# A fused retention, gated MLP and convolution-gate kernel: a third buffer for one tile, other places for weight decoding, and finer first splits

## The chip, the cores and the metric

The kernel runs on one core of one Trainium2 chip. The metric is the device time of one execution in microseconds, as the median of several runs; the profile is one further execution with the hardware profiler. TensorE is called PE here, VectorE DVE, ScalarE ACT, GpSimd POOL and SyncE SP.

## The reference, cut to what matters

Inputs are float32 `q`, `k`, `v` of 8 batches, 8 heads, 576 positions and 64 head dimensions. Weights are handed to the kernel as pairs of 32-bit words of a double. Three layers follow one another (512 model dimensions, feed-forward width 1024):

```
ret = (scale * q @ k.T) * Dmat            # Dmat: gamma[h] ** (i - j) for i >= j, else 0
x   = heads_to_model(ret @ v)             # 8 x 576 x 512

h   = gelu_tanh(x @ w_in);  u, v = halves(h)
v_n = (v - mean) / sqrt(var + 1e-6) * g_ln
v_s = w_sg @ v_n + b_sg                   # mixes the 576 positions of a batch
x   = x + (u * v_s) @ w_out

gate = sigmoid(causal_conv5(x, conv_w));  val = x @ w_val
out  = (gate * val) @ w_out2
```

## The kernel before, in words

**Products.** Every large product is made of three float32r products of a high and a low part (high by high, high by low, low by high), so each operand is "split": ACT copies it into a float32r tile (`hi`, L71), DVE subtracts that from the original (`lo`, L74). A product over 512 model dimensions is 12 matmuls (`product`, L85 to L91).

**First phase, an order written out by a planner.** Up to L901 the program order is the order on every engine (`manual_schedule`, L97). Retention is computed in groups of 192 positions, three to a batch, 24 in all: a burst "o" (`outputs`) and a burst "s" (`scores`, which also calls `adds`). For each batch b there are slow tiles on PE: 4 or 5 tiles "v" (`v_tile`, L435; 12 matmuls of 512 columns; the fifth, s = 4, only in odd batches, carries the last 64 positions of two batches), 8 tiles "u" (`u_tile`, L490; 12 matmuls of 288 columns) and 8 tiles "m" (`mix` and `mix_rest`, L504 to L527; 14 matmuls of 288 columns). The list `slow` (L842 to L854) begins with the v tiles of batches 0 and 1 (nine in a row), and then goes, for b = 0 to 5, through m of batch b, v of batch b + 2, u of batch b + 2. `PLACES` (L33) says ahead of which of these tiles a burst is put. v, u and m tiles share two PSUM buffers (`ps_g`, L110), so PE can begin a tile only when the tile two before it has been read out.

What follows a v tile is a chain over four engines: `v_gelu` (ACT, L446, into a tile `vt`), `v_stat` (DVE L454, L455, then three small POOL instructions L456 to L458 that make `rs`), `v_norm` (ACT L463, in place on `vt`, needs `rs`), `v_high` (ACT L71, into `vh`, or for s = 4 two casts into `vr`) and `v_low` (DVE L74). The pool `two` (L100) gives `vt` two buffers, so the gelu of v tile s + 2 needs `v_low` of tile s done. A u tile is read out by `u_gelu` (ACT L502), an m tile by `gate` (DVE L534, L538).

`plan` (L762) keeps a virtual time `now`: a v tile adds 2.79, a u tile 1.6, an m tile 1.87, and each following step is an event at `now` plus a constant; `work` (L835) sorts the events by time and emits them in that order. `KEYS` (L39) holds the constants; entries 9 to 11 are the offsets of `v_norm`, `v_high` and `v_low` behind the end of their v tile:

```
at(now + 0.1, v_gelu, *args)
at(now + 0.8, v_stat, *args)
for x, f in enumerate((v_norm, v_high, v_low)):
    at(now + KEYS[9 + x], f, *args)
```

**Decoding of the later weights.** Twelve blocks of 128 x 512 doubles (`w_out`, `w_val`, `w_out2`, four each) are decoded two per batch, for batches 2 to 7. `fetch_second` (SP, called at m tile 4 of the batch two before) loads a block into a ring of two `raw` buffers. `decode_at` (L822) is called behind the first u tile: `begin` does the ACT step L128, then there are 4 + 2 + 2 DVE steps (L130 to L143), and a last step, one ACT copy (L146) and SP's write of the decoded block into the DRAM tile `w2d` (L200). The DVE temporaries come from `small_tmp` (L172), where "a" has two buffers and "s" and "t" have one. `KEYS[4]` to `KEYS[8]` set the offsets: both `begin`s at -6 and -5 (in the v tiles), the DVE steps of both blocks from 1.0 on at every 1.5, the last steps at 8 and 12.5. In the same way `split_w_sg` (L865 to L868) splits the five blocks of `w_sg` among the first nine v tiles; `wr`, the fifth, is read by `mix_rest`.

**Second phase, ordered by a scheduler.** From L904 on a list scheduler orders each engine's instructions by its own model. The 4608 positions are cut into nine blocks of 512. `fetch` loads a block of the gated activations (`graw`) and of x (`xraw`), 1 MB each; `split_g` splits the first; `back` is the product with `w_out` and adds x (L939); `split_x` splits the sum; `conv` is the five-tap convolution and the sigmoid (L956 to L961, 16 DVE steps L958 per block); `value` the product with `w_val` (L969), `final` that with `w_out2` (L980). Blocks 0 and 1 are fetched during the last m tiles (batches 6 and 7, L892 to L901), where the piecewise `split_g(0, i)` stands between `mix_rest` and `gate`. `w_out` (`wo`) and then `w_val` and `w_out2` (the halves of `wv`, 2 MB each) are loaded from `w2d` by POOL's queue (L911 to L915). `final` of the last block copies the two halves of a column by ACT and DVE into one tile `o`, each half with a DMA of its own (L986 to L989).

Of the kernel before, what the change touches and what calls it, by code (L numbers as in the profile page):

```python
# [37 lines left out]

KEYS = (13.0, 2.5, 8.0, 2.0, -6.0, 1.0, 1.5, 8, 4.5, 3.9, 4.7, 5.5)  # L39

# [6 lines left out]
def fused_kernel(  # L47
# [48 lines left out]
    with ExitStack() as p1:  # L96
# [75 lines left out]
        def small_tmp(n):  # L172
            return [dec.tile([128, FH], U32, tag=f"d{x}", name=f"d{x}", bufs=2 if x == "a" else 1)[:, :n] for x in "ast"]

# [269 lines left out]
        def v_gelu(b, s):  # L444
            vt = two.tile([128, FH], F32, tag="vt", name="vt")
            act.activation(vt, vs[b, s][0], AF.Gelu_apprx_tanh)  # L446
            vs[b, s] = [vt]
# [314 lines left out]
        def plan(kind, *args):  # L762
# [29 lines left out]
            elif kind == "v":  # L792
                now += 2.79
                at(start, v_tile, *args)
                at(now + 0.1, v_gelu, *args)
                at(now + 0.8, v_stat, *args)
                for x, f in enumerate((v_norm, v_high, v_low)):
                    at(now + KEYS[9 + x], f, *args)
            elif kind == "u":
# [22 lines left out]
        def decode_at(b, place):  # L822
            d = {}

            def begin(j):
                d[j] = decode_second(j)
                run(d[j], 1)

            for n, j in enumerate(jobs(b)):
                at(place + KEYS[4] + n, begin, j)  # L830
                for x in range(3):
                    at(place + KEYS[5] + KEYS[6] * (3 * n + x), lambda j=j, x=x: run(d[j], (4, 2, 2)[x]))
                at(place + KEYS[7] + KEYS[8] * n, lambda j=j: run(d[j]))

# [42 lines left out]
        def fetch(i):  # L877
            g = q_g.tile([128, KT, BLK], F32, tag="graw", name="graw")
            x = q_r.tile([128, KT, BLK], F32, tag="xraw", name="xraw")
            sync.dma_start(out=g, in_=g1d[:, :, i * BLK : (i + 1) * BLK])  # L880
            sync.dma_start(out=x, in_=x1d[:, :, i * BLK : (i + 1) * BLK])
            blk[i] = dict(g=g, x=x)

# [9 lines left out]
        for b in (B - 2, B - 1):  # L893
            for i in range(2 * KT):
                mix(b, i)
                mix_rest(b, i)
                if b == B - 1 and i < KT:
                    split_g(0, i)
                gate(b, i)
                if (b, i) == (B - 1, KT):  # L900
                    fetch(1)  # L901
# [11 lines left out]
    with tc.issue_after(first.ins):  # L913
        for i in range(2):
            pool.dma_start(out=wv[:, i], in_=w2d[:, i + 1])  # L915
    split_g(1)

# [23 lines left out]
    def split_x(i):  # L941
        t = blk[i]
        t["xs"] = q_s.tile([128, 2, KT, BLK], F32R, tag="xs", name="xs")
        for a, z, o in parts(i):
            src = t["x2"][:, :, a + o : z + o]
            hi(act, t["xs"][:, 0, :, a:z], src)
            lo(t["xs"][:, 1, :, a:z], src, t["xs"][:, 0, :, a:z])

# [28 lines left out]
    def final(i, m):  # L977
        t = blk[i]
        ps = ps_2.tile([128, 512], F32, tag="p2", name="ps_out")
        product(ps, BLK, wv[:, 1], slice(m * 128, m * 128 + 128), t["gv"][:, 0], t["gv"][:, 1], slice(0, BLK))  # L980
        o = q_2.tile([128, BLK], F32, tag="o", name="o")
        if i < NBLK - 1:
            act.copy(o, ps[:, :BLK])
            act.dma_start(out=out[:, m, i * BLK : (i + 1) * BLK], in_=o)
            return
        for h, copy, eng in ((0, act.copy, act), (1, dve.tensor_copy, sync)):  # L986
            part = slice(h * BLK // 2, (h + 1) * BLK // 2)
            copy(o[:, part], ps[:, part])
            eng.dma_start(out=out[:, m, i * BLK + part.start : i * BLK + part.stop], in_=o[:, part])  # L989

# [118 lines left out]
```

## Time and profile before

| what | value |
|---|---|
| median of 3 runs | 746.45 us (745.9 to 747.17) |
| the profiled execution's own time | 748.05 us |
| its span in the trace | 746.3 us |
| PE matmul busy | 712.9 us (96%), 7842 matmuls |
| DVE busy | 517.0 us (69%) |
| ACT busy | 331.0 us (44%) |
| POOL busy | 56.4 us (8%) |
| mean granted clock of PE | 0.991 of full speed |
| DMA | 120.93 MB, mean 162 GB/s |

The span is what lies between the first and the last instruction in the trace; the execution's own time has 1.75 us around it. Busy time of PE is modelled: each matmul's bar overlaps the next one's, so a share of 96% says that PE rarely ran dry, not that it worked at its peak. The chain of waits, followed back from the last instruction, runs over PE for 80% of the span, over DVE for 6% and over ACT for 5%.

### The profile page before, as it was taken

How to read it: one execution, taken by the hardware profiler on the slowest of the kernel's cores; microseconds unless marked ns; L12 is line 12 of the kernel's file. 1: busy time of each engine (PE TensorE's matmuls, PEld its weight loads, DVE VectorE, ACT ScalarE, POOL GpSimd, SP SyncE). 2: the span in 40 equal slices, each digit the busy share in tenths (PEclk: the TensorE clock that was granted, in tenths of full speed). 3: DMA queues.
4: the chain of work that ended last, by engine and by line, in shares of the span. 5: the costliest groups of instructions: out<-in, count | busy, mean ns of one | idle time of the engine just before them, and what ended most of it. 6: DMA issues, size and time to landing. Idle time of an engine off the chain costs nothing.

```text
span 746.3 us, 18098 instructions
## 1 busy us (share of the span) xinstructions
PE 712.9 (96%) x7842; PEld 622.4 (83%) x7842; DVE 517.0 (69%) x903; ACT 331.0 (44%) x635; POOL 56.4 (8%) x123
## 2 busy tenths in 40 slices
PE   3799989999999999999999998999999999999997
PEld 3789779898898998998989986888888888888886
DVE  5777678775766765857846569998685958667422
ACT  5666464552643635427345125464352535243221
POOL 0000340300301103001022000000000000000000
PEclk9699999999999999999999999999999999999999
DMA  8969339487079573383531984440422403010111
GB/s 332 354 235 310 125 102 309 177 270 255 6 227 330 171 257 133 139 291 132 163 112 53 399 296 137 146 169 6 164 67 103 141 29 113 1 56 1 56 57 57
DMA packets 54719, 120.93 MB, mean 162 GB/s; under 512 B 3952, under 2 KB 25584, under 8 KB 53872
## 3 DMA queue, kind: packets, MB, share of 16 engines
q1 hardware_dynamic: 36352, 95.13, 37.2%
q10 hardware_dynamic: 17856, 18.35, 6.9%
q0 software_dynamic: 432, 6.29, 2.2%
q8 instruction: 61, 1.00, 0.5%
q14 instruction: 18, 0.15, 0.1%
HBM read 85.16 MB, written 34.60 MB: 160 GB/s over the span
## 4 chain that ended last, share of the span: by engine, by line
PE 80%; DVE 6%; ACT 5%; issue 3%; DMA 2%; POOL 2%; SPq 1%; DVEq 0%; POOLq 0%; ACTq 0%
PE ps_m L516 14%; PE ps_out L91 13%; PE ps_val L91 13%; PE ps_back L91 12%; PE ps_u L91 10%; PE ps_v L429 6%; PE xo L363 2%; DMA qk_sb<-in_qk 2%; PE sc L285 2%; PE xo L355 2%; PE ps_m L524 2%; PE st L301 2%; ACT vt L463 2%; ACT vt L446 1%; DVE stat L454 1%
## 5 line engine op out<-in xcount | busy, mean ns | idle before, releaser
L516 PE MATMUL ps_m<-ws,vh 128*128 128x288 f32 x768 | 113.9, 297 | 0.6 <-DVE gt L534 0.6
L958 DVE SCALAR_TENSOR_TENSOR gate<-x,cw_sb,gate 128x516 f32<-128x516 f32 (+1 forms) x144 | 103.8, 750 | 6.6 <-ACT gate L956 5.3
L516 PEld LDWEIGHTS ps_m<-ws,vh 128*128 128x128 f32 x768 | 105.0, 188 | 1.9 <-DVE gt L534 0.8
L91 PE MATMUL ps_back<-gs,wo 128*128 128x512 f32 x432 | 102.6, 395 | 1.0 <-ACT gs L71 0.6
L91 PE MATMUL ps_val<-xs,wv 128*128 128x512 f32 x432 | 102.5, 395 | 0.9 <-ACT xs L71 0.9
L91 PE MATMUL ps_out<-gv,wv 128*128 128x512 f32 x432 | 102.3, 395 | 0.0
L91 PEld LDWEIGHTS ps_back<-gs,wo 128*128 128x128 f32 x432 | 80.9, 188 | 21.2 <-ACT gs L71 1.1
L91 PEld LDWEIGHTS ps_val<-xs,wv 128*128 128x128 f32 x432 | 81.2, 188 | 20.5 <-ACT xs L71 1.3
L91 PEld LDWEIGHTS ps_out<-gv,wv 128*128 128x128 f32 x432 | 81.3, 188 | 19.2
L91 PE MATMUL ps_u<-xh,wi 128*128 128x288 f32 x448 | 92.9, 297 | 4.0 <-ACT u L502 3.1
L91 PEld LDWEIGHTS ps_u<-xh,wi 128*128 128x128 f32 x448 | 72.6, 188 | 5.9 <-ACT u L502 3.8
L429 PE MATMUL ps_v<-wi,xh 128*128 128x512 f32 x224 | 70.7, 396 | 1.4 <-ACT vt L446 1.4
L91 PE MATMUL ps_u<-xl,wi 128*128 128x288 f32 x224 | 65.9, 294 | 0.0
L973 DVE TENSOR_TENSOR gvf<-ps_val,gate 128x512 f32<-128x512 f32 (+7 forms) x64 | 26.6, 453 | 47.6 <-PE ps_val L91 47.5
L534 DVE SCALAR_TENSOR_TENSOR gt<-ps_m,g_sb,b_sb 128x288 f32<-128x288 f32 x64 | 33.0, 516 | 32.5 <-PE ps_m L524 32.5
L375 ACT COPY xg<-xo 128x768 f32<-128x768 f32 x24 | 19.1, 798 | 77.7 <-PE xo L363 61.4
L71 ACT CAST gv<-gvf 128x512 fp32r<-128x512 f32 x36 | 22.3, 620 | 65.1 <-DVE gvf L973 64.6
L429 PEld LDWEIGHTS ps_v<-wi,xh 128*128 128x128 f32 x224 | 41.5, 188 | 11.2 <-ACT vt L446 1.8
L446 ACT ACTIVATE vt<-ps_v 128x512 f32<-128x512 f32 x36 | 21.5, 598 | 62.1 <-PE ps_v L429 49.4
L956 ACT ACTIVATE gate<-x,cw_sb 128x516 f32<-128x516 f32 (+1 forms) x36 | 25.8, 724 | 47.7 <-DVE x L939 47.6
L265 ACT ACTIVATE kk_sb<-kk_sb,kf_sb 128x64 f32<-128x64 f32 x184 | 46.7, 336 | 0.4 <-DMA kk_sb<-in_kk 0.4
L454 DVE BATCH_NORM_STATS2 stat<-vt 128x6 f32<-128x512 f32 x36 | 25.0, 693 | 31.6 <-ACT vt L446 31.5
(98 smaller groups left out, 1078.9 us busy)
## 6 DMA issues: line engine op xcount, KB each, us to landing
qk_sb<-in_qk SPq DMA_DIRECT2D x24, 960.0 KB, 7.8
vv_sb<-in_vv SPq DMA_DIRECT2D x24, 576.0 KB, 4.6
kk_sb<-in_kk SPq DMA_DIRECT2D x24, 384.0 KB, 5.2
x1d<-xg ACTq DMA_DIRECT2D x24, 384.0 KB, 6.7
g1d<-u SPq DMA_DIRECT2D x16, 576.0 KB, 6.9
graw<-g1d SPq DMA_DIRECT2D x9, 1024.0 KB, 5.9
xraw<-x1d SPq DMA_DIRECT2D x9, 1024.0 KB, 5.3
out<-o ACTq DMA_DIRECT2D x32, 256.0 KB, 2.0
```

The source lines that it names most:

```text
L71: return act.copy(dst, src) if engine is act else engine.tensor_copy(dst, src)
L91: pe.matmul(ps[:, :n], lhs, rhs[:, k, x_cols], start=i == 0, stop=i == last)
L265: act.mul(k[:, j, n], k[:, j, n], kf_sb[:, j, n : n + 1])
L375: act.copy(t["xc"].rearrange("p (o c) n -> p c o n", o=2), t["xo"][:, :, : 2 * GT].rearrange("p c (o n) -> p c o n", o=2),)
L429: pe.matmul(ps, lhs, rhs, start=i == 0, stop=i == KT * 3 - 1)
L446: act.activation(vt, vs[b, s][0], AF.Gelu_apprx_tanh)
L454: dve.bn_stats(stat, vt)
L516: pe.matmul(ps[:, :n], lhs, rhs, start=first, stop=False)
L534: dve.scalar_tensor_tensor(gt, mx.pop((b, i))[:, :n], g_sb[:, m : m + 1], b_sb[:, t0 : t0 + n], op0=ALU.mult, op1=ALU.add)
L956: act.mul(gt, x2[:, m, a:z], cw_sb[:, m, 0:1])
L958: last = dve.scalar_tensor_tensor(gt, x2[:, m, a + j : z + j], cw_sb[:, m, j : j + 1], gt, op0=ALU.mult, op1=ALU.add)
L973: dve.tensor_tensor(gv[:, a:z], ps[:, a:z], t["gate"][:, m, a + o : z + o], op=ALU.mult)
```

## The change

- `vt` gets three buffers for two (2 KB per partition), and the temporary "a" of `small_tmp` one for two (2 KB less).
- The offsets of `v_norm`, `v_high` and `v_low` become 4.1, 4.9 and 5.7; for a batch's last v tile, from batch 2 on, 5.1, 6.0 and 7.0 (`LAST`).
- The two decodings of a batch no longer overlap: block n of a pair has `begin` at 0.5, its DVE steps at 2.0, 3.5 and 5.0 and its last step at 7.5, all plus 8.1 n, counted from the end of the first u tile.
- In the last m tiles `gate` stands ahead of the piecewise `split_g(0, i)`.
- The load of `w_out2` stands in an `issue_after` block on SP's last fetch of block 1; it no longer stands in the one on the load of `w_out`.
- `split_g(1)` and `split_x(0)` work in four pieces of 512 columns each.
- In the last block, the second half of a column goes through a tile of its own (tag "gvf").

```diff
@@ -36,7 +36,8 @@
     ((1, 7, 10), (1, 7, 12)), ((0, 4, 7), (0, 4, 7)),
 ]
 
-KEYS = (13.0, 2.5, 8.0, 2.0, -6.0, 1.0, 1.5, 8, 4.5, 3.9, 4.7, 5.5)
+LAST = (5.1, 6.0, 7.0)
+KEYS = (13.0, 2.5, 8.0, 2.0, 0.5, 2.0, 1.5, 7.5, 8.1, 4.1, 4.9, 5.7)
 
 
 def _as_f32(bits):
@@ -170,7 +171,7 @@
             )
 
         def small_tmp(n):
-            return [dec.tile([128, FH], U32, tag=f"d{x}", name=f"d{x}", bufs=2 if x == "a" else 1)[:, :n] for x in "ast"]
+            return [dec.tile([128, FH], U32, tag=f"d{x}", name=f"d{x}", bufs=1)[:, :n] for x in "ast"]
 
         raws, mx = {}, {}
 
@@ -442,7 +443,7 @@
             vs[b, s] = [ps]
 
         def v_gelu(b, s):
-            vt = two.tile([128, FH], F32, tag="vt", name="vt")
+            vt = two.tile([128, FH], F32, tag="vt", name="vt", bufs=3)
             act.activation(vt, vs[b, s][0], AF.Gelu_apprx_tanh)
             vs[b, s] = [vt]
 
@@ -794,8 +795,9 @@
                 at(start, v_tile, *args)
                 at(now + 0.1, v_gelu, *args)
                 at(now + 0.8, v_stat, *args)
+                last = args[1] == 3 + args[0] % 2 and args[0] > 1
                 for x, f in enumerate((v_norm, v_high, v_low)):
-                    at(now + KEYS[9 + x], f, *args)
+                    at(now + (LAST if last else KEYS[9:])[x], f, *args)
             elif kind == "u":
                 now += 1.6
                 at(start, u_tile, *args)
@@ -827,10 +829,11 @@
                 run(d[j], 1)
 
             for n, j in enumerate(jobs(b)):
-                at(place + KEYS[4] + n, begin, j)
+                p = place + KEYS[8] * n
+                at(p + KEYS[4], begin, j)
                 for x in range(3):
-                    at(place + KEYS[5] + KEYS[6] * (3 * n + x), lambda j=j, x=x: run(d[j], (4, 2, 2)[x]))
-                at(place + KEYS[7] + KEYS[8] * n, lambda j=j: run(d[j]))
+                    at(p + KEYS[5] + KEYS[6] * x, lambda j=j, x=x: run(d[j], (4, 2, 2)[x]))
+                at(p + KEYS[7], lambda j=j: run(d[j]))
 
         def work(lists):
             for kind, *args in lists:
@@ -878,8 +881,8 @@
             g = q_g.tile([128, KT, BLK], F32, tag="graw", name="graw")
             x = q_r.tile([128, KT, BLK], F32, tag="xraw", name="xraw")
             sync.dma_start(out=g, in_=g1d[:, :, i * BLK : (i + 1) * BLK])
-            sync.dma_start(out=x, in_=x1d[:, :, i * BLK : (i + 1) * BLK])
-            blk[i] = dict(g=g, x=x)
+            last = sync.dma_start(out=x, in_=x1d[:, :, i * BLK : (i + 1) * BLK])
+            blk[i] = dict(g=g, x=x, fetched=last.ins)
 
         def split_g(i, k=None):
             t = blk[i]
@@ -894,9 +897,9 @@
             for i in range(2 * KT):
                 mix(b, i)
                 mix_rest(b, i)
+                gate(b, i)
                 if b == B - 1 and i < KT:
                     split_g(0, i)
-                gate(b, i)
                 if (b, i) == (B - 1, KT):
                     fetch(1)
 
@@ -911,9 +914,11 @@
     first = pool.dma_start(out=wo, in_=w2d[:, 0])
     wv = wbig.tile([128, 2, 2, KT, DM], F32R, tag="wbig", name="wv")
     with tc.issue_after(first.ins):
-        for i in range(2):
-            pool.dma_start(out=wv[:, i], in_=w2d[:, i + 1])
-    split_g(1)
+        pool.dma_start(out=wv[:, 0], in_=w2d[:, 1])
+    with tc.issue_after(blk[1]["fetched"]):
+        pool.dma_start(out=wv[:, 1], in_=w2d[:, 2])
+    for k in range(KT):
+        split_g(1, k)
 
     def parts(i):
 
@@ -941,10 +946,11 @@
     def split_x(i):
         t = blk[i]
         t["xs"] = q_s.tile([128, 2, KT, BLK], F32R, tag="xs", name="xs")
-        for a, z, o in parts(i):
-            src = t["x2"][:, :, a + o : z + o]
-            hi(act, t["xs"][:, 0, :, a:z], src)
-            lo(t["xs"][:, 1, :, a:z], src, t["xs"][:, 0, :, a:z])
+        for m in range(KT) if i == 0 else (slice(None),):
+            for a, z, o in parts(i):
+                src = t["x2"][:, m, a + o : z + o]
+                hi(act, t["xs"][:, 0, m, a:z], src)
+                lo(t["xs"][:, 1, m, a:z], src, t["xs"][:, 0, m, a:z])
 
     def conv(i):
         t = blk[i]
@@ -978,15 +984,16 @@
         t = blk[i]
         ps = ps_2.tile([128, 512], F32, tag="p2", name="ps_out")
         product(ps, BLK, wv[:, 1], slice(m * 128, m * 128 + 128), t["gv"][:, 0], t["gv"][:, 1], slice(0, BLK))
-        o = q_2.tile([128, BLK], F32, tag="o", name="o")
         if i < NBLK - 1:
+            o = q_2.tile([128, BLK], F32, tag="o", name="o")
             act.copy(o, ps[:, :BLK])
             act.dma_start(out=out[:, m, i * BLK : (i + 1) * BLK], in_=o)
             return
-        for h, copy, eng in ((0, act.copy, act), (1, dve.tensor_copy, sync)):
+        for h, copy, eng, tag in ((0, act.copy, act, "o"), (1, dve.tensor_copy, sync, "gvf")):
+            o = q_2.tile([128, BLK], F32, tag=tag, name="o")[:, : BLK // 2]
             part = slice(h * BLK // 2, (h + 1) * BLK // 2)
-            copy(o[:, part], ps[:, part])
-            eng.dma_start(out=out[:, m, i * BLK + part.start : i * BLK + part.stop], in_=o[:, part])
+            copy(o, ps[:, part])
+            eng.dma_start(out=out[:, m, i * BLK + part.start : i * BLK + part.stop], in_=o)
 
     for i in range(NBLK + 2):
         if i < NBLK:
```

## Rows read from the trace of the kernel before

**Rows 1.** PE by stage: stretch, its length, PE busy (matmuls), granted clock, DMA share, GB/s.
```profile
76.00:437.50 361.50, 352.93 (x5071) 1.00 0.57 197
437.50:454.00 16.50, 14.57 (x61) 1.00 0.57 203
454.00:742.20 288.20, 288.20 (x1239) 1.00 0.23 79
742.20:746.30 4.10, 0.00 (x1) 1.00 0.38 130
```
**Rows 2.** The same columns of PE, around its interruptions behind 76 us.
```profile
95.00:100.00 5.00, 3.65 (x17) 1.00 0.23 60
105.00:108.00 3.00, 2.01 (x13) 1.00 0.63 197
141.00:143.00 2.00, 1.72 (x13) 1.00 0.00 0
194.00:202.00 8.00, 6.85 (x49) 1.00 0.01 2
243.00:246.00 3.00, 2.47 (x19) 1.00 0.00 0
398.00:401.00 3.00, 1.99 (x15) 1.00 0.00 0
424.00:428.00 4.00, 3.40 (x26) 1.00 1.07 416
447.00:454.00 7.00, 5.07 (x20) 1.00 0.38 130
```
**Rows 3.** Timeline of PE: start us, us, instructions, [idle before <- releaser].
```profile
98.10 0.39 PE L429 MATMUL ps_v<-wi,xl 128*128 128x512 f32 x1
99.84 0.73 PE L429 MATMUL ps_v<-wi,xh 128*128 128x512 f32 x2 [1.35 <-ACT vt L446]
```
**Rows 4.** Waits of ACT, 76 to 440 us: us in total, times, longest.
```profile
ACT vt L446 <- DVE vh L74: 11.8, 16, 2.0
...
ACT vt L463 <- POOL rs L458: 11.3, 13, 1.4
```
**Rows 5.** Timeline of ACT behind the last v tile of batch 7.
```profile
397.95 0.82 ACT L463 ACTIVATE vt<-vt,rs 128x512 f32<-128x512 f32 x1 [1.14 <-POOL rs L458]
398.80 1.26 ACT L71 CAST vr<-vt 64x512 fp32r<-64x512 f32 x2
```
**Rows 6.** POOL's instruction L457 over the whole span: ns min/median/max.
```profile
L457 POOL TENSOR_TENSOR rs<-rs,nh_sb x36: 569/571/1137, 80.9 to 395.9; 128x1 f32<-128x1 f32 x36
```
**Rows 7.** DVE busy in the second decoding of batch 7, and in the second phase's start.
```profile
402.50:406.60 4.10, 3.41 (x7) 1.00 0.34 128
444.00:506.00 62.00, 60.97 (x90) 1.00 0.41 137
```
**Rows 8.** Waits of PE and POOL over the whole span; issues of the block writes, us to landing.
```profile
PE sc L285 <- DMA qk_sb<-in_qk: 9.0, 2, 8.5
...
POOL wv L915 <- DMA w2d<-raw: 13.5, 1, 13.5
...
w2d<-raw SPq DMA_DIRECT2D x12, 512.0 KB, 4.0
```
**Rows 9.** Timeline of ACT in the last m tiles.
```profile
424.54 1.66 ACT L71 CAST gs<-graw 128x512 fp32r<-128x512 f32 x3 [16.42 <-DMA graw<-g1d]
```
**Rows 10.** Tile graw, 400 to 470 us: ns min/median/max of the splits, both shapes.
```profile
L71 ACT CAST gs<-graw x7: 613/622/1909, 424.5 to 468.9; 128x512 fp32r<-128x512 f32 x4, 128x2048 fp32r<-128x2048 f32 x3
L74 DVE TENSOR_TENSOR gs<-graw,gs x6: 684/690/2293, 425.2 to 460.9; 128x512 fp32r<-128x512 f32 x4, 128x2048 fp32r<-128x2048 f32 x2
```
**Rows 11.** Timelines of ACT and of DVE, the split of block 1.
```profile
447.64 1.89 ACT L71 CAST gs<-graw 128x2048 fp32r<-128x2048 f32 x1
...
450.93 2.29 DVE L74 TENSOR_TENSOR gs<-graw,gs 128x2048 fp32r<-128x2048 f32 x1
```
**Rows 12.** Timeline of DVE at the end.
```profile
742.64 0.42 DVE L988 COPY o<-ps_out 128x256 f32<-128x256 f32 x1 [0.81 <-ACT o L988]
```

## The prediction, written before the changed kernel was run

> **What bounds the kernel now.** I read the windows by stage first, then PE's interruptions, then the waits that cause them. PE is the bound: from 454 to 742.2 us it has no gap, 1239 matmuls in 288.2 us, 0.2326 us each, and from 76 to 437.5 us it is idle 361.50 - 352.93 = 8.57 us; the clock is 1.00, the upper level (2.4 GHz), in all of these [rows 1]. The change removes no matmul. It can win only what PE loses in gaps, and the start before 76 us is not touched, since its order is written out and stays.
>
> The gaps are few [rows 2]: 1.35 us near 99, 0.99 near 106, 0.28 near 142, 1.15 between 194 and 202, 0.53 near 244, 1.01 near 399 (one like it lies near 300), 0.60 near 426, and 1.93 between 447 and 454. A gap costs more than its idle time, because bars overlap: at 98.10 the next matmul begins 1.74 later where 0.233 is the pace, so 1.51 is lost for 1.35 idle, and the pair behind it runs 0.73 - 0.39 = 0.34 apart, another 0.11 [rows 3]. I price each interruption at its idle time plus 0.27.
>
> **Third vt buffer, and later offsets.** In the v tiles ACT's gelu waited 16 times for DVE's low part of the tile two before, 11.8 us [rows 4]; when two PSUM tiles are unread, PE stops. That is the gap at 99, and by the timeline also those at 142 and 244, where the first u tiles wait for the last v gelu. With three buffers that gelu waits for the tile three before, 2.8 us more slack than a wait of 2.0 at most. So the wait goes. Next late is the norm, which waited 13 times, 11.3 us, for POOL's `rs` [rows 4], but with another 2.8 us of cover.
>
> The gap at 106 is `wr`, split late on DVE. By the planner's numbers split k stands at 13.9 + 2.79 k = 2.79 (k + 3) + 5.53: behind the low part of tile k + 2 at offset 5.5, ahead of it at 5.7. The last split so no longer sits behind that wait, and I count the gap as gone: 1.35 + 0.99 idle.
>
> The gaps at 202, 300 and 399 are one pattern: behind a batch's last v tile ACT waits 1.14 for `rs`, then runs two casts of 1.26 together, and the u gelus queued behind them free no PSUM [rows 5]. `LAST` puts the norm behind the third u gelu (5.1 against 4.9), about 1.2 us later, by which time `rs` is there, and casts and norm (0.82 + 1.26 = 2.1 us) end about when the fourth u gelu is wanted. Behind the waiting norm stand that gelu and, with it, the sixth u tile; a remnant of 0.1 to 0.3 us each is possible.
>
> Sum here: idle 1.35 + 0.99 + 0.28 + 1.15 + 0.53 + 2 x 1.01 = 6.32, nine interruptions x 0.27 = 2.43, together 8.75. I keep 0.8 back for remnants: **7.95**. Bounds: 8.75, and half of it if another engine inherits the wait. The remaining 8.57 - 6.32 - 0.60 = 1.65 us of gaps I leave as they are.
>
> **Decodings one by one.** Nothing is added; two ACT steps leave the v tiles, and the second block's eight DVE steps (3.4 us [rows 7]) move to 10.1, 11.6 and 13.1 behind the first u tile. The u tiles end at 7 x 1.6 = 11.2, the first m tile at 13.1; its gate stands behind the last two steps, so ends near 13.1 + 1.1 + 0.5 = 14.7, and the third m tile wants its PSUM at 14.9. DVE has nothing else there and will start the steps as soon as the ACT step is done, so I cost it at nothing; without that cover at most about 1 us a batch, six times. On SP the last block write moves from 12.5 to 15.6. It lands 4.0 us after issue [rows 8], about 20, while the next second fetch stands at 18.7 or later (bursts push it) and needs that buffer: SP is held 1 to 2 us, with loads queued behind it. A group's loads are issued two groups ahead, so I cost this at nothing too. One temporary for two: the next `begin` stands behind the copy that frees it, no wait.
>
> **Gate ahead of the pieces.** At 424.54 ACT had waited 16.42 us for the first block's load [rows 9], and DVE's piece stood ahead of the gate that PE needed. Now the gate goes first; the next gate is behind the piece, with one tile of 1.87 us to spare. 0.60 + 0.27 = **0.87**.
>
> **The load of w_out2.** `issue_after` orders only instructions of the named one's own engine; the named one is on SP, the load on POOL. So it does nothing, as far as I read it. Without the old order the load is still last, for POOL waits 13.5 us for the last block write [rows 8]. Cost nothing, gain nothing; were the order kept, block 1 would land sooner, but its split at 447.64 followed ACT work without a wait [rows 11], so between 0 and 0.7.
>
> **First splits in pieces.** Between 447 and 454 PE waits three times, for block 1's ACT split (447.64, 1.89 long), the x split, and DVE's low part (450.93, 2.29 long) [rows 11]: 1.93 + 3 x 0.27 = 2.74. With pieces PE can start on a quarter, 0.62 + 0.69 us after the start [rows 10]. The pieces cost DVE 2 x (4 x 0.690 - 2.293) = 0.93 and ACT 2 x (4 x 0.622 - 1.909) = 1.16 [rows 10]. ACT has room; DVE is busy 60.97 of 62 us behind 444 [rows 7]. I take 2.74 - 0.7 = **2.04**; bounds 2.74 and, if DVE hands its 0.93 on to PE and the split comes no earlier, -0.9. The Trainium skill (Perfetto Trace Analysis, Optimizing Scalar/DVE Operations) speaks against pieces on a full engine: an instruction has some 0.06 us of overhead on DVE, 0.093 on ScalarE. By it six more would cost an estimated 0.36 and 0.56 us, less than the rows say; the sum goes by the rows.
>
> **The end.** DVE's copy started when ACT's into the same tile was done, at 742.64 [rows 12], while PE ended at 742.2 [rows 1]. With two tiles both start together: **0.4**.
>
> **Sum.** 7.95 + 0.87 + 2.04 + 0.4 = 11.26. The profiled execution took 748.05 (span 746.3); 736.8 after, and 1.6 less for the median of the runs, 746.45 - 11.26 = **735.2**.
>
> **Rivals.**
> (a) POOL and DVE inherit the wait in the v tiles, so that half of the 8.75 stays: time 735.2 + 3.6 = 738.8. For it: `rs` waits total 11.3 us, and POOL's L457 takes 0.57 to 1.14 us [rows 6], long where DVE works beside it. Against: three buffers give a whole tile's time. The Trainium skill (SBUF — State Buffer, SBUF: two separate sides) says that a DVE instruction with two SBUF inputs and a GpSimd one exclude each other. By that rule more overlap of low parts with `rs` would make `rs` later; the spread of L457 agrees.
> (b) The second phase is DVE's: the start with 98% gives nothing back, -0.9 in place of 2.04: 738.1. For it: DVE's share. Against: PE had no gap from 454 on at that same share.
> (c) Slower: the late block write holds SP past the lead of the loads, and scores wait for `qk_sb`. One such wait cost about 8.5 us [rows 8]; two take 17 of 11.3: 752. It decides once SP is held longer than the group or so between a load's issue and its use, above some 10 us; I work out 1 to 2.
> (d) The planner's offsets do not carry over and nothing is won but 0.87 and 0.4, less new stalls: about 746.
>
> **Chances.** Forecast 0.74 (732.5 to 737.5), (a) 0.11, (b) 0.08, (c) 0.04, (d) 0.03. The range reaches from everything plus half of the untouched gaps, 746.45 - 12.8 - 0.9 = 732.7, rounded down to 732.3, to past (a) with some loss of (b): 739.8. A measurement here can tell about 0.2%, 1.5 us. Faster by more: forecast, (a), (b), 0.93; within: (d) and a little, 0.03; slower: (c), 0.04.
>
> **What would show it.** Right: no gap near 98, 106, 142, 202, 244, 300 and 399; no ACT wait of L446 for L74; PE without a gap from 438 on; both last copies starting together; the last wv load issued as early as before. Wrong: a PE wait for u or vt there anyway with the norm waiting on `rs`; gates late in the first m tiles; scores waiting for `qk_sb`; a PE gap between 450 and 510 with DVE full.

## The result, and the profile after

The changed kernel takes 735.82 us (median of 4 runs, 734.98 to 736.73), the kernel before 746.81 us beside it (4 runs, 745.9 to 749.37). The ratio is 0.984 with a 95% interval of 0.982 to 0.9861, so it is faster by 1.4 to 1.8%. The forecast was 735.2. The profiled execution took 734.98 us, its span is 733.2; before it was 748.05 and 746.3.

I read the stages of PE first. The columns are those of [rows 1]: stretch, length, PE busy (matmuls), granted clock, DMA share, GB/s.

```profile
75.00:424.50 349.50, 347.73 (x5050) 1.00 0.58 199
424.50:441.00 16.50, 16.50 (x83) 1.00 0.67 238
441.00:729.40 288.40, 288.40 (x1239) 1.00 0.24 83
729.40:733.20 3.80, 0.03 (x1) 1.00 0.30 104
```

PE is still the bound, at the upper clock (2.4 GHz), with the same 7842 matmuls. In the first phase its idle time behind 75 us is 349.50 - 347.73 = 1.77 us, where [rows 1] had 8.57. The stretch round the start of the second phase has no gap at all, where [rows 1] had 16.50 - 14.57 = 1.93. The last 1239 matmuls take 288.40 us, 288.20 before: what was gained behind 437 us was gained at the start of that phase, none of it in its long run.

The same view round the places of [rows 2], each moved by what had been gained up to it:

```profile
94.00:99.00 5.00, 5.00 (x23) 1.00 0.21 59
...
191.00:199.00 8.00, 8.00 (x132) 1.00 0.10 36
...
392.00:395.00 3.00, 3.00 (x25) 1.00 0.00 0
413.00:417.00 4.00, 4.00 (x33) 1.00 1.03 357
437.00:444.00 7.00, 7.00 (x31) 1.00 0.41 135
```

Every one is full, and so are those round 106, 142 and 244 that are left out here. What PE still waits for between 76 and 740 us (us in total, times, longest) is five short waits, none of them at a place of [rows 2]; "issue" is time in which it waited for nothing that the profile shows:

```profile
PE xo L356 <- issue: 0.4, 1, 0.4
PE sc L286 <- issue: 0.4, 1, 0.4
PE ps_v L430 <- ACT xh L72: 0.4, 1, 0.4
PE ps_v L430 <- DVE xl L75: 0.3, 1, 0.3
PE ps_m L517 <- DVE gt L535: 0.2, 1, 0.2
```

The gap at 99 was ACT's gelu waiting for the low part of the tile two before (16 times, 11.8 us in [rows 4]). ACT's waits now, 76 to 430 us:

```profile
ACT vt L447 <- PE ps_v L430: 56.7, 28, 8.6
ACT vt L464 <- POOL rs L459: 6.8, 10, 1.3
```

The gelu waits for the matmuls that feed it, 28 times: ACT is ahead of PE. The wait of the norm for `rs` has shrunk from 11.3 us (13 times) to 6.8 (10 times), and nothing took its place.

By stage, from PE's timelines: the 31st v matmul starts at 82.98 us before and 81.69 after, the first `back` matmul at 437.58 and 427.47, the last matmul ends at 742.2 and 729.4, the span at 746.3 and 733.2. So the first phase, counted from that 31st matmul, went from 354.60 to 345.78, 8.82 less; the second from 304.6 to 301.9, 2.7 less; the end from 4.1 to 3.8, 0.3 less. Another 1.3 us lie ahead of the 31st v matmul, where nothing was changed. Over the thirteen profiles of this study that start takes from 81.0 to 83.0 us (81.09 in `u_last2`, whose first v tiles are those of before, and 82.97 in `u_nolast`), so I put the 1.3 down to that spread. Without it the two profiles differ by 11.8 us, the medians by 11.0.

### The profile page after: what moved, and what is told of

The parts are those of the page before. It is cut to its first block, busy times and chain, and to the rows that moved or that the text cites. A ratio compares the mean times of both kernels' runs of the same rounds, so it can differ in the third digit from the quotient of the medians.

```text
span 733.2 us, 18125 instructions
## 1 busy us (share of the span) xinstructions
PE 708.3 (97%) x7842; PEld 620.8 (85%) x7842; DVE 517.2 (71%) x909; ACT 331.5 (45%) x641; POOL 49.9 (7%) x123
## 4 chain that ended last, share of the span: by engine, by line
PE 92%; DMA 4%; issue 1%; ACT 1%; DVE 1%; SPq 1%; ACTq 0%
PE ps_back L92 14%; PE ps_u L92 14%; PE ps_out L92 14%; PE ps_val L92 14%; PE ps_m L517 14%; PE ps_v L430 13%; PE sc L286 2%; DMA qk_sb<-in_qk 2%; PE xo L364 2%; PE xo L356 2%; PE ps_m L525 2%; PE st L302 2%; DMA x1d<-xg 1%; ACT xg L376 0%; DVE xl L75 0%
## 5 line engine op out<-in xcount | busy, mean ns | idle before, releaser
L92 PE MATMUL ps_u<-xh,wi 128*128 128x288 f32 x448 | 91.4, 296 | 0.0
L430 PE MATMUL ps_v<-wi,xl 128*128 128x512 f32 x112 | 44.3, 396 | 0.3 <-DVE xl L75 0.3
```

The lines of the kernel that those rows point to most:

```text
L92: pe.matmul(ps[:, :n], lhs, rhs[:, k, x_cols], start=i == 0, stop=i == last)
L430: pe.matmul(ps, lhs, rhs, start=i == 0, stop=i == KT * 3 - 1)
```

## The experiments

Seven runs undo a part of the change, or keep one part of several, an eighth (`u_wvdeferred`) does for real what one edit was meant to do; all are measured against the same kernel before. A rerun of the changed kernel itself, with no edit (the run `again`), shows what a median can tell: 734.38 (733.27 to 735.41, 4 runs) where the first was 735.82, and so outside the half microsecond round 735.8 that I expected. Kernels less than about 1.5 us apart are told apart by their traces alone.

> The changed kernel once more, on the same chip as the next one and with more rounds: 735.8, within 0.5; its gaps of PE behind 75 us should be the few small ones again, the largest near 330, where a v tile of batch 6 waits for the parts of x of the retention group just copied out.

To compare places across kernels I take, at each gap of PE, the distance between the starts of the two matmuls on either side of it, less the pace (0.233 us for 512 columns, 0.133 for 288); a dash says that there is none over 0.2 us. The last row is the first phase as above, from the 31st v matmul to the first `back`. All of it is worked out from the timelines, in us:

```
place (us before)     before  after  two     no     no LAST,     LAST   decodings
                                     vt      LAST   old offsets  alone  alone
v tiles, 99           1.51    -      1.51    -      -            1.51   1.50
wr, 106               1.42    -      1.44    -      1.75         1.42   1.42
first u, batch 2      0.44    -      -       -      -            0.44   -
end of v, batch 3     1.47    -      -       -      0.46         0.29   0.85
first u, batch 4      0.69    -      0.68    -      -            0.66   0.66
end of v, batch 5     1.17    -      -       -      0.64         -      0.67
end of v, batch 7     1.17    -      -       -      -            -      -
first phase           354.60  345.78 349.62  344.81 349.18       350.27 351.75
```

**Two buffers again, all else kept (`u_vt2`).**

```diff
-            vt = two.tile([128, FH], F32, tag="vt", name="vt", bufs=3)
+            vt = two.tile([128, FH], F32, tag="vt", name="vt")
-KEYS = (13.0, 2.5, 8.0, 2.0, 0.5, 2.0, 1.5, 7.5, 8.1, 4.1, 4.9, 5.7)
+KEYS = (13.0, 2.5, 8.0, 2.0, 0.5, 2.0, 1.5, 7.5, 8.1, 3.9, 4.7, 5.5)
```

> The changed kernel with two vt buffers again, and with the old offsets 3.9, 4.7 and 5.5 that two buffers need; the later offsets of the last v tile and the decodings one by one stay. My theory (the third buffer is what removes the gelu's wait for DVE's low part): PE's gaps near 99 and 106 and those behind the fourth v tile of batches 2 and 4 come back, 1.35 + 0.99 + 0.28 + 0.53 us idle and some 1.4 us of restarts, about 4.5 us: 740.3. Rival (the ACT steps of the decoding, now out of the v tiles, were what made the gelu late): only 99 and 106 come back, since no decoding runs there, 2.9 us: 738.7. Rival (nothing here hangs on the buffer): 735.8.

Measured: 738.81 us, ratio 0.988 (0.9847 to 0.9912), 3.0 above the changed kernel. Its waits, PE then ACT:

```profile
PE ps_v L430 <- ACT vt L447: 1.3, 1, 1.3
PE ps_m L525 <- DVE wr L72: 0.6, 1, 0.6
PE ps_u L92 <- ACT vt L447: 0.5, 1, 0.5
...
PE ps_m L525 <- DVE wr L75: 0.4, 1, 0.4
...
ACT vt L447 <- DVE vh L75: 14.7, 16, 2.0
```

The gaps at 99, 106 and 244 are back, 1.51 + 1.44 + 0.68 = 3.63 us, and no other of the table, and the first phase is 349.62 - 345.78 = 3.84 us longer: the buffer and its offsets are worth those three places. ACT's 16 waits for the low part are back too (16 times, 11.8 us in [rows 4]), and with three buffers and the old offsets (`u_offsnolast`, next) there is none: this is the wait that the buffer removes. The gaps at 142, 202, 300 and 399 stay away with two buffers: they belong to something else. The median lies at the rival's 738.7, but by places neither expectation holds whole: 244 is back, which the rival left out, and 142 is not, which the theory had.

**No `LAST` (`u_nolast`), and no new offsets at all (`u_offsnolast`), both with three buffers.**

```diff
# u_nolast
-LAST = (5.1, 6.0, 7.0)
+LAST = (4.1, 4.9, 5.7)
# u_offsnolast
-LAST = (5.1, 6.0, 7.0)
+LAST = (3.9, 4.7, 5.5)
-KEYS = (13.0, 2.5, 8.0, 2.0, 0.5, 2.0, 1.5, 7.5, 8.1, 4.1, 4.9, 5.7)
+KEYS = (13.0, 2.5, 8.0, 2.0, 0.5, 2.0, 1.5, 7.5, 8.1, 3.9, 4.7, 5.5)
```

> The changed kernel with the last v tile's three steps at the same offsets as all others (4.1, 4.9, 5.7). My theory: behind the last v tile of batches 3, 5 and 7 ACT again waits for rs and PE loses about 1.28 us each, 3.8 us: 739.6. Rival (with the decoding's DVE steps out of the way rs comes in time, and the later offsets are not needed): 735.8, no gap of PE there.

> The changed kernel with all v tiles at the old offsets 3.9, 4.7 and 5.5, so of the first phase's edits only the third buffer and the decodings one by one are left. My theory: the gap near 99 stays away, that near 106 comes back (1.5 us) because the split of w_sg is again queued behind the low part, and those behind the last v tile of batches 3, 5 and 7 come back (3.8 us): 741.1. Rival (the third buffer and the decoding alone carry the first phase): 735.8 to 736.5.

Measured: 735.44 us without `LAST` (0.9837, 0.9802 to 0.9871), 737.42 without any new offset (0.9854, 0.9814 to 0.9894). In the first PE has four waits between 70 and 460 us, none over 0.3 us. No gap of the table is back, and the first phase is no longer than with it. `LAST` buys nothing that a third buffer, the new offsets and the moved decodings don't buy already. Behind batch 3's last v tile ACT in this kernel reaches the norm without a wait for `rs`:

```profile
192.93 0.81 ACT L464 ACTIVATE vt<-vt,rs 128x512 f32<-128x512 f32 x1
```

Without the offsets PE waits here (two pauses named "issue", 0.9 us each, are left out):

```profile
...
PE ps_m L525 <- DVE wr L72: 0.9, 1, 0.9
...
PE ps_u L92 <- ACT u L503: 0.8, 2, 0.5
...
```

The gap at 106 is there in full (1.75), though 99 is cured, so the later offsets cure it. DVE's order is what the planner's arithmetic had for 5.5 and 5.7, first of this run, then of the changed kernel:

```profile
103.89 0.69 DVE L75 TENSOR_TENSOR vh<-vt,vh 128x512 fp32r<-128x512 f32 x1 [1.44 <-ACT vh L72]
104.50 0.45 DVE L72 CAST wr<-raw 128x576 fp32r<-128x576 f32 x1
```

```profile
99.39 0.46 DVE L72 CAST wr<-raw 128x576 fp32r<-128x576 f32 x1
```

With the old offsets the split of `wr` stands behind a low part that waits for ACT; with the new ones it runs ahead of that wait, about 4 us earlier as counted from the 31st v matmul. And part of the pattern behind odd batches is back (0.46 and 0.64), through the u gelus: 0.2 us of offset matters there as well.

**`LAST` alone, and the new decodings alone, both with two buffers and the old offsets (`u_last2`, `u_decalone`).**

```diff
# u_last2: LAST stays, the rest of the first phase but the gate is as before
-            vt = two.tile([128, FH], F32, tag="vt", name="vt", bufs=3)
+            vt = two.tile([128, FH], F32, tag="vt", name="vt")
-KEYS = (13.0, 2.5, 8.0, 2.0, 0.5, 2.0, 1.5, 7.5, 8.1, 4.1, 4.9, 5.7)
+KEYS = (13.0, 2.5, 8.0, 2.0, -6.0, 1.0, 1.5, 8, 4.5, 3.9, 4.7, 5.5)
-                p = place + KEYS[8] * n
-                at(p + KEYS[4], begin, j)
+                at(place + KEYS[4] + n, begin, j)
...
# u_decalone: the decodings stay
-LAST = (5.1, 6.0, 7.0)
+LAST = (3.9, 4.7, 5.5)
-KEYS = (13.0, 2.5, 8.0, 2.0, 0.5, 2.0, 1.5, 7.5, 8.1, 4.1, 4.9, 5.7)
+KEYS = (13.0, 2.5, 8.0, 2.0, 0.5, 2.0, 1.5, 7.5, 8.1, 3.9, 4.7, 5.5)
-            vt = two.tile([128, FH], F32, tag="vt", name="vt", bufs=3)
+            vt = two.tile([128, FH], F32, tag="vt", name="vt")
```

> The changed kernel with two vt buffers, the old offsets and the old overlapping decodings, but with the later offsets 5.1, 6.0 and 7.0 of a batch's last v tile: of the first phase's edits these alone are left. What it settles: the gaps of 1.28 us behind the last v tile of batches 3, 5 and 7 were gone in the run with two buffers, which had these offsets and the new decodings, and were also gone in the run without the offsets. My theory (offsets or decodings, either is enough): no gap near 200, 300 and 399; the gaps near 99, 106, 142 and 244 are there (1.62 + 1.53 + 0.54 + 0.79 = 4.5 us): 740.3. Rival (only the decodings' new place removes them): three gaps of 1.28 come back as well: 744.1.

> The changed kernel with two vt buffers and the old offsets for every v tile, so that of the first phase's edits the decodings one by one alone are left. The run with three buffers and otherwise the same had gaps of 0.46 and 0.64 us behind the last v tile of batches 3 and 5. My theory now (the decodings' new place removes most of those gaps, since ACT's two steps and DVE's first four stood ahead of rs and the norm): gaps of 0.4 to 0.7 in batches 3, 5 and 7, and those near 99, 106 and 244 as with two buffers, 3.9 us: 740.5. Rival (it was the third buffer, and the decodings did nothing): three gaps of 1.28 and that near 142 come back: 743.5.

Measured: 740.28 us (0.9904, 0.988 to 0.9929) and 741.69 (0.9922, 0.9898 to 0.9947). Both have the gap at 99 with the wait that the third buffer removes (1.3 us idle, as in `u_vt2`). The next longest wait of PE in `u_last2` is one of the second phase:

```profile
PE ps_back L92 <- ACT gs L72: 0.9, 1, 0.9
```

The last two columns of the table are the point of the pair. The gap of 0.44 at 142 goes with the decodings (it is there with `LAST` alone): before, their two ACT steps (L128, at 137.13 and 138.18) lay in the v tiles, on either side of the cast whose low part the next gelu waits for, and none of their DVE steps had begun. Behind batches 3, 5 and 7 each of the two parts alone removes something, `LAST` 1.18, 1.17 and 1.17, the decodings 0.62, 0.50 and 1.17. The parts overlap. With two buffers and the old offsets, `LAST` and the decodings together leave no gap there (`u_vt2`); with three buffers and the new offsets the decodings leave none without `LAST` (`u_nolast`). `LAST` with the third buffer but the old decodings was not tried, since the two don't fit in SBUF together.

`u_decalone` and `u_offsnolast` differ by the third buffer alone. It takes away 99 and 244 and about half of the gap behind batch 3 (0.85 to 0.46), little behind batch 5 (0.67 to 0.64), and leaves 106. ACT's 16 waits of the gelu for the low part (14.7 us) go, but the norm's waits for `rs` grow, first with two buffers, then with three:

```profile
ACT vt L464 <- POOL rs L459: 6.7, 11, 1.3
...
ACT vt L464 <- POOL rs L459: 11.8, 10, 2.9
```

So part of the wait is handed on to POOL's `rs`, as rival (a) feared; the later offsets take that away again (7.5 us in `u_nolast`, 6.8 in the changed kernel). Put in order, the first phase falls from 354.60 to 351.75 us with the decodings and the gate, to 349.18 with the buffer and to 344.81 with the offsets; `LAST`, last, adds nothing (345.78).

That wait of `u_last2` is a surprise: the pieces are in it, and PE still waits 0.9 us for the split of block 1. That its median, 740.28, meets the theory's 740.3 is so in part luck: the second phase is 303.07 us, 1.1 more than in the changed kernel. ACT there, and in the changed kernel:

```profile
441.26 0.63 ACT L966 ACTIVATE gate<-gate 128x512 f32<-128x512 f32 x1 [0.83 <-DVE gate L963]
441.86 0.62 ACT L72 CAST xs<-x 128x512 fp32r<-128x512 f32 x1
442.38 0.72 ACT L961 ACTIVATE gate<-x,cw_sb 128x512 f32<-128x512 f32 x1
443.01 2.17 ACT L72 CAST gs<-graw 128x512 fp32r<-128x512 f32 x4
```

```profile
437.36 0.63 ACT L967 ACTIVATE gate<-gate 128x512 f32<-128x512 f32 x1 [0.82 <-DVE gate L964]
437.90 2.17 ACT L72 CAST gs<-graw 128x512 fp32r<-128x512 f32 x4
```

In the changed kernel those four casts stand directly behind the sigmoid, here the scheduler put a cast for `xs` and a conv step ahead of them. What the pieces give hangs also on where the scheduler puts them.

**Whole first splits again (`u_whole`).**

```diff
-    for k in range(KT):
-        split_g(1, k)
+    split_g(1)
-        for m in range(KT) if i == 0 else (slice(None),):
+        for m in (slice(None),):
```

> The changed kernel with the first splits of block 1 and of x of block 0 whole again. My theory: PE waits again two or three times between the first back and value products, 1.93 us idle, 2.7 us with restarts: 738.5. Rival (it was the gate's place or the third buffer that let the splits come earlier, the scheduler then finds a place for whole ones too): 735.8.

Measured: 737.42 us (0.9863, 0.9831 to 0.9896), 1.6 above the changed kernel; from the first `back` matmul to the last matmul 305.6 us for 301.9 to 302.0. PE's timeline of it, and then a window with PE busy and the granted clock in the columns:

```profile
438.63 1.20 PE L92 MATMUL ps_back<-gs,wo 128*128 128x512 f32 x4 [0.63 <-ACT gs L72]
440.73 1.81 PE L92 MATMUL ps_val<-xs,wv 128*128 128x512 f32 x4 [0.90 <-ACT xs L72]
442.34 4.00 PE L92 MATMUL ps_back<-gs,wo 128*128 128x512 f32 x12
```

```profile
440.70:444.40 3.70, 3.67 (x9) 0.55 0.87 285
```

The first two of the three gaps of before are back as they were (0.63 and 0.90 idle, both named for the splits; [rows 11] has the casts). They cost 0.79 + 1.06 us, and the matmul behind each another 0.10, 2.06 in all by the timeline. The third gap is not there as a wait. The rest of the 3.64, about 1.6, lies behind the second gap: in a stretch of 3.7 us the clock is 0.55 and matmuls are 0.43 us apart in place of 0.232, that is, PE runs at the lower level (1.2 GHz) for most of it. The pieces are so worth about 2.1 us by the gaps, and the rest goes by the clock. In the changed kernel PE runs through:

```profile
427.47 12.29 PE L92 MATMUL ps_back<-gs,wo 128*128 128x512 f32 x52
439.60 4.82 PE L92 MATMUL ps_val<-xs,wv 128*128 128x512 f32 x20
```

The gap was closed in two ways: `back` of block 1 starts on a quarter of its operands (the last 4 of the 52 matmuls), and the scheduler puts 20 matmuls of `val` ahead of the rest of it. What each of the two is worth was not tried. The Trainium skill (Perfetto Trace Analysis, Optimizing Scalar/DVE Operations) says that where ScalarE or VectorE isn't saturated but causes bubbles on other engines, breaking up its instructions may let work be completed sooner. This pair of runs agrees, with about 2.1 us: both gaps are named for ACT's casts, and ACT was busy 34.85 of the 62 us behind 444 in the kernel before.

**The gate behind the pieces again (`u_gate`).**

```diff
-                gate(b, i)
                 if b == B - 1 and i < KT:
                     split_g(0, i)
+                gate(b, i)
```

> The changed kernel with the piecewise split of block 0 ahead of the gate again. My theory: the gate of the first m tile of batch 7 waits behind DVE's piece for the load of block 0 and PE loses about 0.87 us once, near 415: 736.7. Rival (PE is now ahead or the load earlier, so that the piece is not late): 735.8, no gap. The scheduler may also order the second phase otherwise; a gap of PE there is told apart by its place.

Measured: 735.16 us (0.9833, 0.9806 to 0.986), not told apart from the changed kernel by time. The trace has the step, PE and DVE:

```profile
416.76 1.46 PE L517 MATMUL ps_m<-ws,vh 128*128 128x288 f32 x9 [0.92 <-DVE gt L535]
```

```profile
415.58 0.69 DVE L75 TENSOR_TENSOR gs<-graw,gs 128x512 fp32r<-128x512 f32 x1 [2.42 <-ACT gs L72]
416.19 0.51 DVE L535 SCALAR_TENSOR_TENSOR gt<-ps_m,g_sb,b_sb 128x288 f32<-128x288 f32 x1
```

DVE stands idle for 2.42 us, waiting for the piece's cast (which had itself waited 15.81 us for the load of block 0), and does the piece first. The gate, whose matmuls were done near 414, so starts at 416.19, and PE loses 1.08 us, start to start and less the pace. The theory holds. The part is worth about that in the trace, though a median can't show it, nor the first phase as a whole: 345.51 us here, 344.81 in `u_nolast`, but also 345.78 in the first profile of the changed kernel, which had 1.3 us of the pauses told of in the last section.

**The load of `w_out2` really held back (`u_wvdeferred`).** On SP's own queue the order binds.

```diff
     with tc.issue_after(blk[1]["fetched"]):
-        pool.dma_start(out=wv[:, 1], in_=w2d[:, 2])
+        sync.dma_start(out=wv[:, 1].bitcast(F32), in_=w2d[:, 2])
```

> The changed kernel with the load of w_out2 on SP's queue, really behind the last fetch of block 1 (in the changed kernel the order binds nothing: the program with the old order has the same instructions in the same order on each engine). My theory: block 1 lands some us earlier, but its split is placed by the scheduler behind ACT's other work and PE has no gap there to give back: 735.8, within 0.5. Rival (PE or DVE was held by block 1's load): 0.5 to 2 us faster. Other rival (SP waits for the last block write and holds the fetches behind it): slower, with PE waiting in the first products.

Measured: 735.4 us (0.9838, 0.9806 to 0.987). First, of the changed kernel, the issue of the load, SP's last fetch of block 1 and the fetch of its `graw` (us from issue to landing at the end of the row), then, of this one, the issue, ACT's split of block 1 and the same fetch:

```profile
413.25 0.54 POOL L919 DMA_DIRECT2D wv<-w2d  x1 [13.09 <-DMA w2d<-raw]
...
424.59 1.41 SPq L884 DMA_DIRECT2D xraw<-x1d  x1
...
graw<-g1d SPq DMA_DIRECT2D x1, 1024.0 KB, 11.1
```

```profile
423.79 0.80 SPq L919 DMA_DIRECT2D wv<-w2d  x1
...
437.82 2.17 ACT L72 CAST gs<-graw 128x512 fp32r<-128x512 f32 x4
...
graw<-g1d SPq DMA_DIRECT2D x1, 1024.0 KB, 6.2
```

In the changed kernel POOL issued the load at 413.25, as soon as the last block write had landed, with a wait of 13.09 us (13.5 in [rows 8]), and 11.3 us ahead of the fetch that `issue_after` names: the block moved nothing. Issued 10.5 us later for good, the load leaves room for block 1's `graw` (6.2 us to landing, 11.1 in the changed kernel), but ACT's split starts at 437.82 in place of 437.90: it follows ACT's own work, not the load. Held back or not, it is worth nothing here.

**A step further: the last gaps (`y_place`, `y_both`).** In the first phase the changed kernel kept gaps near 330 us, where the split of batch 6's x (`xh`, `xl`) came late for its v tiles. `y_place` puts two bursts ahead of earlier tiles, by two and by one. `y_both` adds, in the last block, a product of its own for each half of the last column, in a PSUM tile of its own.

```diff
# y_place, in PLACES
-    ((1, 7, 10), (1, 7, 12)), ((0, 4, 7), (0, 4, 7)),
+    ((1, 5, 9), (1, 7, 12)), ((0, 4, 7), (0, 4, 7)),
# y_both besides, in final, ahead of its product
+        if i == NBLK - 1 and m == KT - 1:
+            for h, copy, eng, tag in ((0, act.copy, act, "o"), (1, dve.tensor_copy, sync, "gvf")):
+                part = slice(h * BLK // 2, (h + 1) * BLK // 2)
+                ps = ps_2.tile([128, 512], F32, tag="p2", name="ps_out")
+                product(ps, BLK // 2, wv[:, 1], slice(m * 128, m * 128 + 128), t["gv"][:, 0], t["gv"][:, 1], part)
...
```

> The changed kernel with the second and third output bursts of batch 6 earlier in the list of slow tiles (places 5 and 9 for 7 and 10), so that the high and low parts of x are there when the fourth v tile of batch 6 wants them. My theory: the gap near 330 goes, 0.4 us idle and 0.7 to 1.35 with restarts: 735.0. Rival (the wait moves to the copy-out, which has one buffer and waits for its own write to DRAM, or to the burst's products that wait for DVE's masking): no change or up to 1 us slower.

> The changed kernel with the places of batch 4's xl/xh moved as in the run y_place, and the last block's last column computed as two products of 256 columns in two PSUM tiles of their own, each copied out by one engine. Theory (the two copies of the end are in a row because they read one PSUM tile): with two tiles DVE's copy waits only for PE and starts within 0.1 us of PE's end instead of 0.4 us later, ACT's copy of the first half lies under the second half's matmuls, and PE's end to the span's end falls from 3.8 us to 3.4 to 3.5; median 733.2 (0.3 less than y_place). Rival (the end is the output DMA's own time, or 24 matmuls of 256 columns cost PE what the copies save): PE's end to the span's end stays at 3.7 or more, or the last column takes over 0.2 us longer on PE; median 733.5 or more, up to 734.

Measured: `y_place` 733.49 us (0.9824, 0.9797 to 0.9851), `y_both` 734.06 (0.9808, 0.978 to 0.9837), the changed kernel 734.38 on the chip of `y_place` (`again`). The waits of `xh` and `xl` are gone in `y_place` (what is left of PE's list is one row, `xo`, 0.3 us of "issue"); that is 0.4 to 1.0 us in the profiles, and the times don't tell it from nothing. The end, first of the changed kernel, then of `y_both`:

```profile
729.46 0.37 ACT L995 COPY o<-ps_out 128x256 f32<-128x256 f32 x1 [1.41 <-PE ps_out L92]
729.87 0.42 DVE L995 COPY o<-ps_out 128x256 f32<-128x256 f32 x1 [1.19 <-ACT o L995]
```

```profile
729.23 0.42 DVE L991 COPY o<-ps_out 128x256 f32<-128x256 f32 x1
729.35 0.37 ACT L991 COPY o<-ps_out 128x256 f32<-128x256 f32 x1 [0.61 <-DMA out<-o]
```

With two PSUM tiles the copies run side by side, so they had stood in a row for their common PSUM tile: the theory's mechanism is right. Its gain isn't there. ACT's copy now waits 0.61 us for an earlier output transfer to give its `o` buffer back, and from PE's end (729.0) to the end of the span (733.0) it takes 4.0 us, 3.8 in the changed kernel. The rival's outcome holds. Neither version is shown to be faster than the changed kernel.

## Why the prediction was right, step by step

The sum was 11.26 us; the medians differ by 746.81 - 735.82 = 10.99. The forecast's case happened. Its terms against the traces:

- **v tiles, 7.95, and gate, 0.87: together 8.82; the first phase is 8.82 shorter.** That the two agree to the last digit is luck, since two profiles of the changed kernel differ by a microsecond there (345.78 and 344.79). All places are full, and the wait of [rows 4] was the cause at 99 and 244, the offset at 106. The pricing of a gap at idle time plus 0.27 was a little high: idle time fell by 8.57 - 1.77 = 6.80, the phase by 8.82, so the ten restarts that I had counted took 2.02, 0.20 each. The 0.8 kept back for remnants was not needed in its place, and covered that.
- **Which part does what was wrong in three places.** I gave the gap at 142 to the third buffer; it stays away with two. I gave the gaps behind odd batches to `LAST`; without it they stay away (`u_nolast`), because the buffer, the offsets and the decodings get there first. And I costed the decodings at nothing: I named the two ACT steps that leave the v tiles, but priced only the place that the DVE steps move to. Moved alone, the decodings are worth 0.44 + 0.62 + 0.50 + 1.17 = 2.7 us (`u_decalone` against before). That the ACT steps did it is shown at 142 only; behind the odd batches their DVE steps moved too, and the two were not taken apart. The sum did not suffer, since I had counted the gaps and not the parts. A forecast for `LAST` on top of the rest would have been wrong by all that I gave it, 3.17 us of idle time and its restarts.
- **The decodings' cover.** Right in the main: no wait of PE over 0.4 us is left between 76 and 740, and none for a load of scores. But a late gate in the first m tiles, one of my signs of being wrong, is there once, near 159, where the kernel before has none: 0.2 us idle, 0.4 start to start. DVE there, in the changed kernel:

```profile
157.56 0.96 DVE L75 TENSOR_TENSOR xl<-xg,xh 128x768 fp32r<-128x768 f32 x1 [1.39 <-ACT xh L72]
158.44 0.51 DVE L535 SCALAR_TENSOR_TENSOR gt<-ps_m,g_sb,b_sb 128x288 f32<-128x288 f32 x1
```

  The gate stands behind the low part of x, not behind a decoding, and it is late with the old decodings too (0.5 us in `u_last2`), so it doesn't hang on the moved DVE steps.
- **`w_out2`, nothing.** Right twice over: the order binds nothing, and a real delay wins nothing either.
- **Pieces, 2.04; the second phase is 2.7 shorter, and `u_whole` gives back 2.1 in gaps.** The upper bound, 2.74, was nearer. The step that failed is the 0.7 taken off for DVE's 0.93. First, DVE is still full there, 60.72 of the 62 us behind 434 (60.97 behind 444 in [rows 7]), but it hands nothing on, for PE runs on from 424.5 without a gap. Being full was not being late. Second, the 0.93 was too high, because I added up the bars of the pieces, and bars overlap on DVE as on PE. DVE in the changed kernel, then the instruction behind the whole split of [rows 11]:

```profile
440.74 1.89 DVE L75 TENSOR_TENSOR gs<-graw,gs 128x512 fp32r<-128x512 f32 x3
442.54 0.74 DVE L964 SCALAR_TENSOR_TENSOR gate<-x,cw_sb,gate 128x512 f32<-128x512 f32 x1
```

```profile
453.13 0.75 DVE L958 SCALAR_TENSOR_TENSOR gate<-x,cw_sb,gate 128x512 f32<-128x512 f32 x1
```

  From start to start a piece takes 1.80 / 3 = 0.60, four take 2.40, and the whole split took 453.13 - 450.93 = 2.20: 0.2 for each of the two splits, 0.4 in place of 0.93. ACT's 1.16 shrinks in the same way, to about 0.5 (four casts take 2.07 from start to start, the whole split 1.81).
- **The end, 0.4; 0.3 gained, but not by my step.** I expected both copies to start together with two SBUF tiles. DVE still waits for ACT's copy, since the two read one PSUM tile, and where they don't (`y_both`) the span's end isn't nearer. The 0.3 is more than scatter: eleven profiles with the changed end take 3.7 to 3.8 us from PE's end, the one of before 4.1. By the issues, the last two transfers start as long behind PE's end as before (0.44 and 0.89 us) but land 1.7 us later in place of 2.2 and 2.0, and ACT's copy of the column ahead waited 0.96 us for a buffer in place of 1.50. So the extra tile sends the transfers ahead of the last ones out sooner; that this is why the last ones land sooner was not tried.
- **Rivals.** (a), another engine inheriting the wait: in the changed kernel POOL's `rs` waits fell, so no; but the mechanism is real, for with the third buffer and the old offsets they stood at 11.8 us, 6.7 without the buffer, and it is the offsets that cover it. (b), a second phase bound by DVE: no gap in it. (c), SP held: no wait for `qk_sb` or a load. (d), no gain: refuted by the table.

A small slip besides: the low end of the range, 732.3, doesn't follow from the 732.7 that it is worked out from.

Not settled: what the third buffer and the offsets would do behind the odd batches without the moved decodings, since these don't fit together; and the 1.3 us of the start, which I call spread because the order there is the same and the profiles scatter by 2.0, without having isolated it.

## What to carry to other kernels

Count the gaps of the engine that is the bound, price each with its restart, and ask of each which engine's instruction stood ahead of the late one: a gain predicted by places holds even where several parts of a change cover the same place, a gain predicted by parts does not. A step that is moved also frees the place that it leaves, and that belongs in its price as much as the place it moves to. Price pieces of an instruction, like gaps, from start to start: summed bars count their overlap twice. Two SBUF tiles did not make two engines' copies independent here while they read one PSUM tile.

## What was not expected of the hardware

- In `u_whole`, PE ran at the upper clock up to its second gap (0.63 and 0.90 us idle, 2.1 us apart), then at 0.55 for 3.7 us, which cost about 1.6 us more. The kernel before has the same two gaps (0.64 and 0.90, up to 449.59 and 451.68) and stays at 1.00 [rows 1]. Gaps of this size can so cost half the clock for a while, and need not; what decides I can't say from these runs.
- PE pauses within bursts of 64 x 64 matmuls for no reason that the trace shows ("issue"). They are there in every profile, mostly in the same two bursts (near 125 and near 165) and of other sizes from one to the next: by the table's measure 1.37 us at 169 before, 0.66 at 123 and 0.64 at 164 after. They bound what a single profile can tell to about a microsecond.
